# Down projections moved in between the two parts of the input projection, and a last output tile split over two PSUM tiles

## The chip, the cores and the metric

The kernel runs on one NeuronCore of a Trainium2 chip. The metric is the device time of one execution in microseconds (us), the median of several executions on the chip. The profile of one execution gives the start and the length of every instruction on each engine: TensorE (PE, the matmuls; PEld is its weight load), VectorE (DVE), ScalarE (ACT), GpSimd (POOL) and SyncE (SP, which issues most DMAs).

## The reference, cut to what matters

The input x has 2048 tokens of 448 features. It is normalised; one branch is a linear recurrence over the tokens (a diagonal complex state), the other a gated feed-forward layer; the output joins them.

```python
xn = _layernorm(x, axis=-1)
# branch s: Bu = xn @ B_bar (complex); h_t = Lam_bar * h_{t-1} + Bu_t
y = 2.0 * einsum("blp,dp->bld", hseq, Cmat).real + xn * Dskip     # = s
# branch g: w_gate, w_up are 448 x 1792, w_down is 1792 x 448
h = sigmoid(xn @ w_gate) * (xn @ w_up)
g = silu(h @ w_down)
return x + s * g
```

## The kernel before, in words

**Tiling.** The tokens are cut into four chunks c of 512; each chunk has four output tiles j of 128 tokens. Per chunk PE does four kinds of work:

- gate and up (`gu_step`, L688 and L689): 14 steps, one for each of seven 256-wide blocks of w_gate and w_up. The 448 features are contracted as seven slices of 64 rows, and two 64-row matmuls run side by side on the two halves of the array, into the two halves of one `gu` tile. ACT turns a gate tile into `sig` (L702), DVE joins the up tile with it into `hF` (L705).
- the input projection of the recurrence (`b_units`), for four blocks pt of state, taken two at a time. 448 is 3 x 128 + 64, so each block has a 64-row part, the *pairs* (L736 and L737, for pt 3 L739 and L741), and three full-row parts for each of the real and the imaginary half, the *fulls* (L749, L752). All of them add up in one `gu` tile; ACT copies it to `bus` (L760 to L768), and DVE runs the scan on it (`ssm_pair`, L796 to L820; `ssm_stack`, L830 to L850), which gives `hT`.
- the down projection (`down`, L864): 14 full-row matmuls of 448 columns over `hF` of the chunk before, into an `acc` tile; ACT makes `g_t` of it (L870).
- the output of the recurrence (`yout`, L889): seven full-row matmuls over `hT`; then DVE adds the skip term (L895), multiplies with `g_t` (L897), adds x (L899), and SP stores the tile (L901).

Down and output of chunk c - 1 are spread among the gate and up steps of chunk c; those of the last chunk come at the end.

**PSUM.** There are three `gu` tiles of two 2 KB halves each (one for each index of their middle dimension), handed out in turn by `next_gu`, and two `acc` tiles of one half each, handed out in turn by `next_acc`. At the end, when gate and up are through, the six halves of the three `gu` tiles are handed out singly as `free_banks`, the two halves of one tile after each other.

**Order.** Every operation is added to a planner (`Plan`) with an estimated cost and with what it reads and writes. PE's order is that of the program, exactly. For the other engines the planner works out backwards from PE's order when each operation is due, then goes forwards and takes, of what is available, the operation that is due first. So the orders of ACT, DVE, POOL and SP come out of the costs, and they come out anew when PE's order or a cost is changed. Instructions on one engine run in the order in which they were emitted. `SW`, 0.1 us, is the planner's cost of a change between 64-row and full-row matmuls on PE; `first=True` of `down` adds it.

**Names that the change touches.** `b_units(c, pts)` adds one PE operation for the pairs of both blocks, then one for the fulls of each with its ACT copies. `down(c, j, first, bank)` adds one PE operation and the `g_t` operation. `yout(c, j, first, banks, parts)` can cut its 448 columns into parts, each with its own matmuls, DVE operations and store. The calls touched stand in chunk 1 (L974 to L979), chunk 2 (L992 to L998), chunk 3 (L1013 to L1019) and at the very end (L1046). Chunk 0's `b_units` have no `down` to go with.

Of the kernel before, what the change touches and what calls it, by code (L numbers as in the profile page):

```python
# [73 lines left out]
class Plan:  # L74
# [10 lines left out]
    def add(self, eng, cost, fn, r=(), w=(), dma=0, lat=None, chain=False, name="", rate=230e3):  # L85
        o = Op()
        o.idx, o.eng, o.cost, o.fn, o.dma, o.name = len(self.ops), eng, cost, fn, dma, name
        o.lat = LAT.get(eng, 0.0) if lat is None else lat
        o.pre, o.suc, o.rate = {}, [], rate
        o.slot = None  # L90
        if dma and eng != "POOL":
            o.slot, self.n_dma = self.n_dma, self.n_dma + 1
        o.start = o.end = None
        for k in r:
            if k in self.w:
                self._edge(self.w[k], o, True)
        for k in w:
            for q in self.r.get(k, ()):
                self._edge(q, o, False)
            if k in self.w:  # L100
                self._edge(self.w[k], o, True)
        for k in w:
            self.w[k] = o
            self.r[k] = []
        for k in r:
            if k not in w:
                self.r.setdefault(k, []).append(o)
        if chain or eng == "PE" or (eng == "DVE" and self.seq):
            key = ("chain", eng)
            if key in self.last_of:  # L110
                self._edge(self.last_of[key], o, None)
            self.last_of[key] = o
        self.ops.append(o)
        return o
# [131 lines left out]
def kernel(  # L246
# [95 lines left out]
    acc = [pp.tile([P, 512], FP32, name=f"acc{i}") for i in range(2)]  # L342

    pl = Plan(185.0)
    add = pl.add
# [121 lines left out]
    def next_acc():  # L467
        a = acc_n[0] % 2
        acc_n[0] += 1
        return a  # L470
# [29 lines left out]
    def xr(c, lo=0, hi=TPC):  # L500
        return [("xnT", c % 3, j, h) for j in range(lo, hi) for h in "ab"]
# [176 lines left out]
    SW = 0.1  # L678
# [44 lines left out]

    bus_n = [0]

    def b_units(c, pts, last_r=True):
        x = xnT[c % 3]
        slots = [next_gu() for _ in pts]
        bk = [("bT", 0), ("bT", 1), ("bT3", 0), ("bT3", 1), "bT3l"] + (
            [("bT6", 0), ("bT6", 1)] + [("bT6", i, h) for i in range(2) for h in range(2)] if 3 in pts else [])  # L730

        def pairs():
            for pt, a in zip(pts, slots):
                if pt < 3:
                    ps = slice(pt * P, pt * P + P)
                    T.matmul(gu[a][:, 0, :], lhsT=bT[0:H, 3, 0, ps], rhs=x[0:H, 6, :], start=True, stop=False)  # L736
                    T.matmul(gu[a][:, 1, :], lhsT=bT[H:P, 3, 1, ps], rhs=x[H:P, 5, :], start=True, stop=False)  # L737
                else:
                    T.matmul(gu[a][:, 0, 0:256], lhsT=bT6[0:H, 3, :], rhs=x[0:H, 6, 0:256],  # L739
                             start=True, stop=False)  # L740
                    T.matmul(gu[a][:, 1, 0:256], lhsT=bT6[H:P, 3, :], rhs=x[H:P, 5, 256:512],  # L741
                             start=True, stop=False)
        add("PE", 0.216 * len(pts), pairs, r=xr(c) + bk, w=[("gu", a) for a in slots], name=f"bp{c}.{pts[0]}")
        for n, (pt, a) in enumerate(zip(pts, slots)):
            def fulls(pt=pt, a=a):
                for i in range(2):
                    for kt in range(3):
                        if pt < 3:
                            T.matmul(gu[a][:, i, :], lhsT=bT[:, kt, i, pt * P:pt * P + P], rhs=x[:, 2 * kt, :],  # L749
                                     start=False, stop=(kt == 2))  # L750
                        else:
                            T.matmul(gu[a][:, i, 0:256], lhsT=bT6[:, kt, :],  # L752
                                     rhs=x[:, 2 * kt, i * 256:i * 256 + 256], start=False, stop=(kt == 2))
            add("PE", (6 * 0.215 if pt < 3 else 6 * 0.11) + (0 if n else SW), fulls,
                r=xr(c) + bk + [("gu", a)], w=[("gu", a)], name=f"b{c}.{pt}")
            u = bus_n[0] % NBUS
            bus_n[0] += 1
            bus_of[c, pt] = u
            if pt < 3:
                add("ACT", act(1024), lambda u=u, a=a: A.copy(out=bus[u][:], in_=gu[a][:]),  # L760
                    r=[("gu", a)], w=[("bus", u)])
            else:
                h2 = lambda t: t.rearrange("p (i n) -> p i n", i=2)
                add("ACT", act(512), lambda u=u, a=a: A.copy(out=h2(bus[u][:, 0, :]), in_=gu[a][:, :, 0:256]),
                    r=[("gu", a)], w=[("bus", u)])
                add("ACT", 0.6, lambda u=u, a=a: A.copy(out=h2(bus[u][0:H, 1, :]), in_=gu[a][H:P, :, 0:256]),
                    r=[("gu", a)], w=[("bus", u, 1)])
                add("ACT", 0.6, lambda u=u, a=a: A.copy(out=h2(bus[u][H:P, 1, :]), in_=gu[a][0:H, :, 0:256]),  # L768
                    r=[("gu", a)], w=[("bus", u, 2)])
# [87 lines left out]
    def down(c, j, first=False, bank=None):  # L857
        key, d = bank if bank else (lambda a: (("acc", a), acc[a][:, 0:D]))(next_acc())
        js = slice(j * P, j * P + P)

        def f():
            for ft in range(FT):
                m, h = ft % 7, ft // 7
                T.matmul(d, lhsT=hF[c % 2][:, m, h, js], rhs=wd[:, ft, :], start=(ft == 0), stop=(ft == FT - 1))  # L864
        add("PE", 14 * 0.189 + (SW if first else 0), f, r=[("wd", 0), ("wd", 1)] + [("hF", c % 2, m) for m in range(7)], w=[key],
            name=f"d{c}.{j}")
        g = gt_n[0] % NGT
        gt_n[0] += 1
        gt_of[c, j] = g
        add("ACT", act(448), lambda: A.activation(g_t[g][:], d, ACT.Silu, scale=0.5), r=[key, "silutab"], w=[("gt", g)])  # L870
# [4 lines left out]
    def yout(c, j, first=False, banks=None, parts=((0, D),)):  # L875
        js = slice(j * P, j * P + P)
        t = c * TPC + j
        g = gt_of[c, j]
        o = o_n[0] % NO
        o_n[0] += 1  # L880
        q = t % NXD
        xq = xd[q][:]
        for pi, (c0, c1) in enumerate(parts):
            key, y = banks[pi] if banks else (lambda a: (("acc", a), acc[a][:, 0:D]))(next_acc())
            y = y[:, 0:c1 - c0]

            def f(y=y, c0=c0, c1=c1):
                for i, (hm, cm) in enumerate(K_ORDER):
                    T.matmul(y, lhsT=hT[c % 2][:, hm, js], rhs=cT[:, cm, c0:c1], start=(i == 0), stop=(i == 6))  # L889
            n = c1 - c0  # L890
            add("PE", 7 * (0.004 + n / 2400.0) + (SW if first else 0), f,
                r=cTk + [("hT", c % 2, p) for p in range(4)], w=[key], name=f"y{c}.{j}")
            ok = ("o", o, pi)
            od = o_t[o][:, c0:c1]
            add("DVE", dve1(n), lambda od=od, y=y, c0=c0, c1=c1: V.tensor_tensor(out=od, in0=y, in1=xq[:, c0:c1], op=ALU.add),  # L895
                r=[key, ("xd", q)], w=[ok])
            add("DVE", dve2(n), lambda od=od, c0=c0, c1=c1: V.tensor_tensor(out=od, in0=od, in1=g_t[g][:, c0:c1], op=ALU.mult),  # L897
                r=[ok, ("gt", g)], w=[ok])
            add("DVE", dve2(n), lambda od=od, c0=c0, c1=c1: V.tensor_tensor(out=od, in0=od, in1=x_all[:, t, c0:c1], op=ALU.add),  # L899
                r=[ok, ("x", t)], w=[ok])  # L900
            add("SP", 0.45, lambda od=od, c0=c0, c1=c1: Q.dma_start(out=out_flat[t * P:(t + 1) * P, c0:c1], in_=od),  # L901
                r=[ok], w=[("store", t, pi)], dma=n * 256)
# [68 lines left out]
    halves(1, 2)  # L971
    gu_step(1, 2)
    prepare(2)
    b_units(1, (0, 1))  # L974
    down(0, 0)
    for i in range(3, 6):
        gu_step(1, i, i == 3)
    b_units(1, (2, 3))
    down(0, 1)  # L979
    for i in range(6, 12):  # L980
        gu_step(1, i, i == 6)
    down(0, 2, True)
# [6 lines left out]

    for i in range(0, 4):  # L990
        gu_step(2, i)
    b_units(2, (0, 1))  # L992
    down(1, 0)
    yout(0, 2)
    for i in range(4, 7):
        gu_step(2, i, i == 4)
    b_units(2, (2, 3))
    down(1, 1)  # L998
    yout(0, 3)
    prepare(3)  # L1000
    for i in range(7, 12):
# [8 lines left out]

    for i in range(0, 4):
        gu_step(3, i)
    b_units(3, (0, 1))  # L1013
    down(2, 0)
    yout(1, 2)
    for i in range(4, 7):
        gu_step(3, i, i == 4)
    b_units(3, (2, 3))
    down(2, 1)  # L1019
    yout(1, 3)  # L1020
    for i in range(7, 12):
        gu_step(3, i, i == 7)
# [20 lines left out]
    down(3, 2, bank=free_banks[2])  # L1043
    yout(3, 2)
    down(3, 3, bank=free_banks[3])
    yout(3, 3, banks=[free_banks[4], free_banks[5]], parts=((0, 256), (256, 448)))  # L1046

    pl.solve({"g0.0": 5.9})
    with tc.manual_schedule():
# [33 lines left out]
```

## Time and profile before

| | |
|---|---|
| median of 4 runs | 190.05 us (189.2 to 190.36) |
| the profiled execution | 189.6 us, its span (first to last instruction) 187.8 us |
| granted TensorE clock, mean | 0.998 |
| PE busy | 181.1 us, 96% of the span |
| DVE busy | 168.4 us, 90% |
| ACT busy | 87.6 us, 47% |
| POOL busy | 32.7 us, 17% |

How to read it: PE's matmuls overlap, so that the length printed for one (0.38 us for 512 columns) is longer than the distance to the next (0.22 us); sums are made with the distances. "x14" in a row is a merged run of 14 instructions. The share of busy time is a mean over the span; which engine sets the end has to be read from the chain of waits and from the idle time in front of the instructions. In a row, "[0.20 <-DVE hF L705]" means that the engine stood idle for 0.20 us before it and that this ended with an operation of DVE's line 705.

### The profile page before, as it was taken

To read this page: it belongs to the slowest core of one execution; us is meant where nothing else is said; L and a number is where in the kernel's file an instruction comes from. 1 tells how busy PE (TensorE), PEld (TensorE's weight loads), DVE (VectorE), ACT (ScalarE), POOL (GpSimd) and SP (SyncE) were. 2 spreads that over 40 slices of the span, in tenths; PEclk is the share of its full clock that TensorE was granted. 3 is DMA by queue.
4 is the path that set the end of the run, shared out by engine and by line. 5 is a ranking of instruction groups with operands and counts; after the bars stand their busy time and mean duration, and the time that the engine had idled before them with its cause. 6 is when DMAs were issued, how large, how long until landed. Compare 5 with 4: busy or idle time off the path is not lost.

```text
span 187.8 us, 3507 instructions
## 1 busy us (share of the span) xinstructions
PE 181.1 (96%) x1375; PEld 89.8 (48%) x1375; DVE 168.4 (90%) x303; ACT 87.6 (47%) x124; POOL 32.7 (17%) x84
## 2 busy tenths in 40 slices
PE   7999999999999999999999999999999999999990
PEld 2585554474454444444454445444445445455560
DVE  3765799997999999999999998999999999899943
ACT  3469997734988751244547331237146221502110
POOL 3163466000005560000027800000000000000000
PEclk9999999999999999999999999999999999999999
DMA  5999999599500033200000343000000100000220
GB/s 126 266 217 239 167 140 210 112 249 130 187 3 0 0 72 78 49 0 3 0 2 0 77 101 70 0 28 0 24 3 0 49 0 28 0 24 28 73 77 24
DMA packets 29239, 13.43 MB, mean 71 GB/s; under 512 B 19619, under 2 KB 29222, under 8 KB 29222
## 3 DMA queue, kind: packets, MB, share of 16 engines
q1 hardware_dynamic: 27878, 12.05, 31.6%
q10 hardware_dynamic: 1344, 1.15, 2.3%
q8 instruction: 11, 0.18, 0.4%
q14 instruction: 6, 0.05, 0.1%
HBM read 6.77 MB, written 1.84 MB: 46 GB/s over the span
## 4 chain that ended last, share of the span: by engine, by line
PE 80%; DMA 8%; DVE 7%; issue 1%; POOL 1%; SPq 1%; ACT 1%; DVEq 0%
PE gu L688 33%; PE acc L864 17%; PE acc L889 11%; PE gu L749 9%; PE gu L864 6%; DMA x_all<-in_A_x_dram 5%; DVE hF L705 3%; DMA wG<-in_B_w_gate_dram 3%; PE gu L752 1%; PE gu L736 1%; DVE bst L421 1%; SPq L351 1%; POOL sdb L436 1%; PE gu L889 1%; PE gu L689 1%
## 5 line engine op out<-in xcount | busy, mean ns | idle before, releaser
L688 PE MATMUL gu<-xnT,wG 64*128 64x512 bf16 (+1 forms) x224 | 46.4, 349 | 0.3 <-DVE xnT L489 0.3
L689 PE MATMUL gu<-xnT,wG 64*128 64x512 bf16 (+1 forms) x224 | 46.4, 350 | 0.0
L688 PE MATMUL gu<-xnT,wU 64*128 64x512 bf16 (+1 forms) x203 | 46.2, 369 | 0.2 <-ACT sig L702 0.2
L689 PE MATMUL gu<-xnT,wU 64*128 64x512 bf16 (+1 forms) x203 | 46.2, 369 | 0.0
L702 ACT ACTIVATE sig<-gu 128x1024 f32<-128x1024 f32 x21 | 21.3, 1021 | 32.0 <-PE gu L689 29.7
L864 PE MATMUL acc<-wd,hF 128*128 128x448 bf16 x168 | 33.8, 353 | 0.0
L864 PEld LDWEIGHTS <-hF 128*128 128x128 bf16 x224 | 21.7, 98 | 20.9 <-issue 1.3
L688 PEld LDWEIGHTS <-wG 64*128 64x128 bf16 x224 | 20.4, 94 | 21.1 <-issue 3.0
L688 PEld LDWEIGHTS <-wU 64*128 64x128 bf16 x203 | 18.8, 94 | 22.1 <-issue 1.3
L705 DVE SCALAR_TENSOR_TENSOR hF<-sig,gu 128x1024 bf16<-128x1024 f32 x21 | 25.5, 1214 | 1.5 <-PE gu L689 1.1
L803 DVE TENSOR_TENSOR_SCAN wv<-c_r,st,z 128x512 bf16<-128x512 f32 x18 | 23.0, 1275 | 0.0
L889 PE MATMUL acc<-cT,hT 128*128 128x448 bf16 x105 | 22.0, 353 | 0.0
L689 PEld LDWEIGHTS <-wG 64*128 64x128 bf16 x224 | 20.3, 94 | 0.2
L689 PEld LDWEIGHTS <-wU 64*128 64x128 bf16 x203 | 18.7, 94 | 0.5 <-issue 0.5
L749 PE MATMUL gu<-xnT,bT 128*128 128x512 bf16 x72 | 16.9, 380 | 0.0
L760 ACT CAST bus<-gu 128x1024 bf16<-128x1024 f32 x12 | 12.1, 1010 | 9.3 <-PE gu L749 9.0
L889 PEld LDWEIGHTS <-hT 128*128 128x128 bf16 x119 | 11.5, 98 | 10.1 <-issue 0.4
L870 ACT ACTIVATE g_t<-acc 128x448 bf16<-128x448 f32 x12 | 6.5, 538 | 17.6 <-PE acc L864 17.6
L435 POOL TENSOR_SCALAR veb<-mv 128x2 bf16<-128x2 bf16 (+1 forms) x5 | 3.8, 754 | 55.3 <-DVE mv L422 55.2
L421 DVE BATCH_NORM_STATS2 bst<-x_all 128x6 f32<-128x448 bf16 x16 | 9.4, 613 | 3.6 <-DMA x_all<-in_A_x_dram 3.6
L454 ACT ACTIVATE xn<-x_all,nmr,rsd 128x448 bf16<-128x448 bf16 x12 | 8.4, 764 | 6.0 <-POOL nmr L444 5.9
L864 PE MATMUL gu<-wd,hF 128*128 128x448 bf16 x56 | 11.1, 352 | 0.0
(132 smaller groups left out, 245.4 us busy)
## 6 DMA issues: line engine op xcount, KB each, us to landing
out_dram<-o_t SPq DMA_DIRECT2D x15, 112.0 KB, 1.7
wd<-in_B_w_down_dram SPq DMA_DIRECT2D x2, 784.0 KB, 5.5
x_all<-in_A_x_dram SPq DMA_DIRECT2D x3, 448.0 KB, 4.5
wU<-in_B_w_up_dram SPq DMA_DIRECT2D x2, 448.0 KB, 11.4
wU<-in_B_w_up_dram SPq DMA_DIRECT2D x2, 336.0 KB, 7.1
wG<-in_B_w_gate_dram SPq DMA_DIRECT2D x1, 448.0 KB, 8.3
wG<-in_B_w_gate_dram ACTq DMA_DIRECT2D x1, 448.0 KB
xnT<-xn SPq DMA_TRANSPOSE x24, 2.4
```

The source lines that it names most:

```text
L421: add("DVE", 0.6, lambda: V.bn_stats(out=bst[b][:], in_=x_all[:, t, :]), r=[("x", t)], w=[("bst", b)])
L454: add("ACT", 0.65, lambda: A.activation(xn[b][:, 0:448], x_all[:, t, :], ACT.Identity, bias=nmr[:, t, :], scale=rsd[:, t, :]), r=[("x", t) ...
L688: T.matmul(gu[a][:, 0, ts], lhsT=w_[0:H, s, ms], rhs=x[0:H, s, ts], start=(s == 0), stop=(s == 6))
L689: T.matmul(gu[a][:, 1, ts], lhsT=w_[H:P, (s + 1) % 7, ms], rhs=x[H:P, s, ts], start=(s == 0), stop=(s == 6))
L702: add("ACT", act(1024), lambda: A.activation(th, gu[a][:], ACT.Tanh, scale=0.5), r=[("gu", a)], w=[tk])
L705: add("DVE", dve1(1024), lambda: V.scalar_tensor_tensor(out=ho, in0=th, scalar=1.0, in1=gu[a][:], op0=ALU.add, op1=ALU.mult), r=[("gu", a) ...
L749: T.matmul(gu[a][:, i, :], lhsT=bT[:, kt, i, pt * P:pt * P + P], rhs=x[:, 2 * kt, :], start=False, stop=(kt == 2))
L760: add("ACT", act(1024), lambda u=u, a=a: A.copy(out=bus[u][:], in_=gu[a][:]), r=[("gu", a)], w=[("bus", u)])
L803: dve(1.194, lambda k=k: V.tensor_tensor_scan(out=wv[:, k, :], data0=rb, data1=z[:, k, :], initial=(st[pt][:, k, :] if c else 0.0), op0=AL ...
L864: T.matmul(d, lhsT=hF[c % 2][:, m, h, js], rhs=wd[:, ft, :], start=(ft == 0), stop=(ft == FT - 1))
L870: add("ACT", act(448), lambda: A.activation(g_t[g][:], d, ACT.Silu, scale=0.5), r=[key, "silutab"], w=[("gt", g)])
L889: T.matmul(y, lhsT=hT[c % 2][:, hm, js], rhs=cT[:, cm, c0:c1], start=(i == 0), stop=(i == 6))
```

## The change

`b_units` takes a function `mid` and calls it between the pairs and the fulls. In chunks 1, 2 and 3 the two `down` calls that stood behind `b_units` become this `mid`. Between the pairs and the fulls of the same blocks there are then 14 full-row matmuls into an `acc` tile; the planner's cost of the mode change goes from the first fulls to this `down`. An argument that nothing used goes away. The outputs `yout` that stand behind a `down` in chunks 2 and 3 stay where they are, behind the fulls.

Apart from that, the very last output tile: its two parts were columns 0 to 255 and 256 to 447 in the two halves of one `gu` tile; they become columns 0 to 127 in the next `acc` tile and columns 128 to 447 in the first half of that `gu` tile.

```diff
-    def b_units(c, pts, last_r=True):
+    def b_units(c, pts, mid=None):
...
         add("PE", 0.216 * len(pts), pairs, r=xr(c) + bk, w=[("gu", a) for a in slots], name=f"bp{c}.{pts[0]}")
+        if mid:
+            mid()
         for n, (pt, a) in enumerate(zip(pts, slots)):
...
-            add("PE", (6 * 0.215 if pt < 3 else 6 * 0.11) + (0 if n else SW), fulls,
+            add("PE", (6 * 0.215 if pt < 3 else 6 * 0.11) + (0 if n or mid else SW), fulls,
...
-    b_units(1, (0, 1))
-    down(0, 0)
+    b_units(1, (0, 1), lambda: down(0, 0, True))
     for i in range(3, 6):
         gu_step(1, i, i == 3)
-    b_units(1, (2, 3))
-    down(0, 1)
+    b_units(1, (2, 3), lambda: down(0, 1, True))
...
-    b_units(2, (0, 1))
-    down(1, 0)
+    b_units(2, (0, 1), lambda: down(1, 0, True))
     yout(0, 2)
...
-    b_units(2, (2, 3))
-    down(1, 1)
+    b_units(2, (2, 3), lambda: down(1, 1, True))
     yout(0, 3)
...
-    b_units(3, (0, 1))
-    down(2, 0)
+    b_units(3, (0, 1), lambda: down(2, 0, True))
     yout(1, 2)
...
-    b_units(3, (2, 3))
-    down(2, 1)
+    b_units(3, (2, 3), lambda: down(2, 1, True))
     yout(1, 3)
...
-    yout(3, 3, banks=[free_banks[4], free_banks[5]], parts=((0, 256), (256, 448)))
+    a = next_acc()
+    yout(3, 3, banks=[(("acc", a), acc[a]), free_banks[4]], parts=((0, 128), (128, 448)))
```

## The prediction

> **What bounds the kernel now.** First the page's busy line, then the sum of PE's waits.
>
> ```profile
> PE 181.1 (96%) x1375; PEld 89.8 (48%) x1375; DVE 168.4 (90%) x303; ACT 87.6 (47%) x124; POOL 32.7 (17%) x84
> ```
> ```profile
> PE gu L736 <- DVE hF L705: 0.5, 2, 0.3
> PE gu L688 <- ACT sig L702: 0.2, 1, 0.2
> ```
>
> Past the first 10 us PE has 0.7 us of waits in all: it sets the pace, and only something that shortens PE's own stream, or what comes behind its last matmul, can shorten the kernel. So the third view is the end of the chain of waits, and the timeline beside it.
>
> ```profile
> 179.23 2.65 PE gu L864 x14
> 181.88 1.36 PE gu L889 x14
> 183.26 0.44 DVE o_t L895
> 183.79 0.30 DVE o_t L897
> 184.11 0.29 DVE o_t L899
> 184.41 0.28 DVE o_t L895
> 184.71 0.27 DVE o_t L897
> 185.00 0.26 DVE o_t L899
> ```
> ```profile
> 172.65 0.98 ACT L870 ACTIVATE g_t<-gu 128x448 bf16<-128x448 f32 x2 [8.47 <-PE gu L864]
> ...
> 179.36 0.62 DVE L895 TENSOR_TENSOR o_t<-acc,xd 128x448 bf16<-128x448 f32 x1
> ...
> 181.72 1.51 PE L889 MATMUL gu<-cT,hT 128*128 128x256 bf16 x14
> ...
> 183.26 0.42 DVE L895 TENSOR_TENSOR o_t<-gu,xd 128x256 bf16<-128x256 f32 x1 [2.36 <-PE gu L889]
> ```
>
> The reader is to see that DVE, idle for 2.36 us, takes up part one of the last tile only when *both* parts' 14 matmuls are through, and then does six operations in a row (183.26 to 185.26) with nothing beside them.
>
> **Part two of the change, the last tile.** Is that wait due to the shared tile? Two other rows say so: the two `g_t` of downs (3,0) and (3,1), also in two halves of one `gu` tile, both start at 172.65, when the second down is through; and L895 of tile (3,2), in a tile of its own, starts at 179.36 while PE is already 0.3 us into the next down. Here a rule speaks against the change: the Trainium skill ("PSUM — Partial Sum Buffer", Summary: rules for kernel authors) asks of a read during matmuls only that it be in a different bank. The halves already are two banks, so by the rule DVE could start early now and the new tile brings 0. The rows show the wait at tile grain; I follow them.
>
> The sum needs three durations at new widths. Matmul distance: 448 columns 2.65 / 14 = 0.189 us; 256 columns 0.109 (the starts 8.20, 8.31, 8.41 of the first gate step); a line through both gives 0.136 at 320 and 0.056 at 128 (six 128-column transposes in 0.51 us, the last one 0.24 of it: 0.054). L895: 0.62 at 448, 0.42 at 256, 0.35 at 192, so 0.28 at 128 and 0.49 at 320. L897 and L899: 0.38, 0.29, 0.26, so 0.23 and 0.32. Between dependent DVE operations lie 0.03 to 0.04, and 0.11 after part one's L895.
>
> - PE: part one 181.72 + 7 x 0.056 = 182.11; part two + 7 x 0.136 = 183.06. Now it is 181.72 + 7 x 0.109 + 7 x 0.083, 183.06 too, as the columns are as many. DVE starts 0.20 later (183.26).
> - DVE, part one: 182.31, + 0.28 + 0.11 + 0.23 + 0.03 + 0.23 = 183.19, all beside part two's matmuls. `g_t`, needed at 182.70, is there at 181.91 + 0.54 = 182.45.
> - DVE, part two: 183.26, when PE releases it; + 0.49 + 0.04 + 0.32 + 0.03 + 0.32 = 184.46. Now 185.26: **0.80 earlier**.
> - The last store is 80 KB instead of 48 KB. The DMA rows give 1.5 us from issue to landing for 48 KB, 1.6 for 64, 1.7 for 112: **0.1 later**. A second rule: "DMA: Bandwidth & Descriptors" (Specifications) wants 512 B per descriptor at least; rows of the last store go from 384 B to 640 B, so the rule would make it cheaper, while the rows show a longer landing with more bytes across that line. I take the rows. Part one's store (32 KB) is issued at about 183.2 and SP is free of it 0.33 us later, before 184.46.
>
> Sum: -0.70 us, with -0.55 if L895's release takes longer, -0.8 if the landing doesn't grow.
>
> **Part one of the change, the moved downs.** From the timeline of chunk 2:
>
> ```profile
> 84.11 0.38 PE L736 MATMUL gu<-xnT,bT 64*128 64x512 bf16 x1
> ...
> 84.33 0.38 PE L736 MATMUL gu<-xnT,bT 64*128 64x512 bf16 x1
> ...
> 84.64 2.76 PE L749 MATMUL gu<-xnT,bT 128*128 128x512 bf16 x12
> ...
> 87.24 2.81 PE L864 MATMUL acc<-wd,hF 128*128 128x448 bf16 x14
> ...
> 89.89 1.49 PE L889 MATMUL acc<-cT,hT 128*128 128x448 bf16 x7
> ```
>
> Pair to pair is 0.22, pair to full 0.31: the change of mode costs 0.09, once. A down behind 64-row matmuls pays the same elsewhere: the chain has 2.75 for those and 2.65 for a down behind full rows. So the 0.09 moves from the fulls to the down; after it all stay full-row, and the way back into 64 rows is paid once, as now. Six places times 0. The 12 fulls take 2.60 = 12 x 0.217, with no hole between a pair and the full that adds to the same half: no stall that the down could fill. PE's stream gets no shorter.
>
> Waits that the new places could add:
> - *The down, 2.6 us earlier* (2.0 in the second groups). It needs all seven `hF`: the last L705 of each chunk before ends at 38.99, 80.03 and 122.9, the new downs start at 42.8, 84.6 and 128.0. Covered by 3.8 us or more. Their `g_t` on ACT come earlier; ACT is busy 47%.
> - *The fulls, 2.65 us later*, and so their ACT copies. They free the `gu` tiles. Tightest is chunk 1's second group, with no output tile behind: fulls of 1.30 and 0.65, then gate and up steps of 1.51. The second step reuses pt 2's tile 2.25 us after its fulls (mode change included), and the copy takes 0.2 + 1.0; the third reuses pt 3's 3.1 us after its own, and its three copies (0.59, 0.58, 0.58) are done some 2.4 after. Cover 0.7 to 1.0 us. ACT has other work there (two 0.6 us `wv` copies, a 0.67 us `ctmp`); if the planner puts one of these first, PE waits 0 to 0.5 us, once.
> - *The scan on DVE reads `bus`.* In chunks 1 and 2 the first new `bus` (ready at 45.3 and 87.2) waits 25 and 14 us for its L796 (70.9 and 101.8), whatever the delay. In chunk 3 it is close: the first copy ends at 130.51 and is read at 133.75. 2.65 later it ends at 133.16: cover 0.6 us.
>
> ```profile
> 129.50 1.01 ACT L760 CAST bus<-gu 128x1024 bf16<-128x1024 f32 x1 [1.04 <-PE gu L749]
> ...
> 133.75 0.69 DVE L796 TENSOR_TENSOR ta<-bus,cosT 128x1024 bf16<-128x1024 bf16 x1
> ```
>
> What if it is not covered? DVE's backlog ends at L895 of tile (2,2), 171.51 to 172.13, whose `acc` tile PE needs at 172.45: about 0.25 us, plus 0.54 that DVE stood idle before L705 at 164.67. DVE can lose 0.8 us before PE waits.
>
> Both ends for the moved downs: +0.5 (a chunk-1 wait) and -0.4 (the stalls at 42.47 and 108.72, 0.2 each, gone by a new order; the one at 30.3 lies before the first moved step). I take 0, the row being a stream without holes.
>
> **Sum:** 189.6 - 0.7 = 188.9 for an execution like the profiled one. That one lies 0.45 below the median of the runs, so on their median **189.35**, say 189.3.
>
> **Rivals.**
> 1. *The order drawn anew also loses the two 0.2 us stalls:* -1.1, 188.95. For it: those are orders of ACT and DVE that came out badly and are worked out again. Against: as many can come in.
> 2. *Slower: DVE starves in chunk 3.* All `bus` tiles of that chunk come 2.65 us later and DVE's order is fixed; if it stands idle that long in front of L796, 2.65 - 0.8 = 1.85 reaches PE at tile (3,0), less 0.7 from the tail: +1.15, 191.2. It decides once DVE loses more than 1.5 us. For it: DVE is busy 90% and has holes of only some 1.1 us between 130 and 170. Against: the cover of 0.6, and work of chunk 2 that can go first.
> 3. *Part two's DVE work waits for part one's store,* as both lie in one `o_t` tile: the store lands at about 184.75, then 1.20 on DVE, so 185.95 instead of 185.26, +0.1 for the bytes: +0.8, 190.85. Against: the statistics of the first x tile start at 3.14 while another transfer into the same x_all, issued at 1.2 and 2.7 under way, is in flight; but that is a read behind a write, not a write behind a read.
> 4. *The tile isn't what part one waits for:* the six operations stay in a row, 190.05.
>
> **How the numbers follow.** Forecast (tail alone) 0.49; rival 1 0.25; rival 2 0.13; rival 3 0.08; rival 4 0.05. The median of four runs spans 0.6%, so 0.5%, 0.95 us, is about what can be told from no change. The forecast's -0.7 lies within it; with 0.4 us either way from the new order, more than a third of its chance lies beyond. Faster: 0.19 + 0.21 = 0.40. Slower: rival 2 and half of rival 3 and a little, 0.18. The same: 0.42. The range goes from 188.4 (rival 1 with 0.5 more) to 190.9 (rival 3), which leaves out rival 2.
>
> **What would show it.** Right: L895 of the last tile starts near 182.3 on the old time axis for part one and right behind PE's last matmul for part two, L901's last issue is 0.8 us earlier measured from PE's last matmul; 0.31 from pair to down, 0.19 from down to full. Wrong: idle DVE before L796 of chunk 3, PE waits on ACT's L760 to L768 in chunk 1, part two's L895 starting with a landing of L901, or PE's last matmul at another time than 183 by more than 0.5 us.

## The result, and the profile after

The changed kernel takes 189.14 us (median of 37 executions), the kernel before 189.81 us (median of 56; the 190.05 shown ahead was that of the first four). The ratio is 0.9971, with a 95% interval from 0.9957 to 0.9984: 0.3% faster, between 0.3 and 0.8 us. The profiled execution took 189.17 us, its span is 187.4 us.

In the changed source the lines behind `b_units` have moved down by two: L749 is L751, L864 is L866, L889 is L891, L895 to L901 are L897 to L903. First PE's waits in the changed kernel, without the 1.2 us in front of its first matmul, then the end of its chain of waits.

```profile
PE gu L688 <- DMA wG<-in_B_w_gate_dram: 0.5, 1, 0.5
PE gu L688 <- ACT sig L702: 0.2, 1, 0.2
PE gu L736 <- DVE hF L705: 0.2, 1, 0.2
```
```profile
179.51 2.65 PE gu L866 x14
182.16 0.39 PE acc L891 x7
182.55 0.96 PE gu L891 x7
183.54 0.50 DVE o_t L897
184.07 0.34 DVE o_t L899
184.43 0.32 DVE o_t L901
```

Three DVE operations instead of six lie behind the last matmul. The timeline shows where the other three went (start, length, operation, and in brackets the idle time before):

```profile
182.00 0.55 PE L891 MATMUL acc<-cT,hT 128*128 128x128 bf16 x7
...
182.39 1.11 PE L891 MATMUL gu<-cT,hT 128*128 128x320 bf16 x7
182.59 0.29 DVE L897 TENSOR_TENSOR o_t<-acc,xd 128x128 bf16<-128x128 f32 x1 [1.05 <-PE acc L891]
182.99 0.23 DVE L899 TENSOR_TENSOR o_t<-o_t,g_t 128x128 bf16<-128x128 bf16 x1
183.25 0.22 DVE L901 TENSOR_TENSOR o_t<-o_t,x_all 128x128 bf16<-128x128 bf16 x1
183.54 0.49 DVE L897 TENSOR_TENSOR o_t<-gu,xd 128x320 bf16<-128x320 f32 x1
```

Part one's L897 starts 0.59 us after the tile's first matmul (before: 1.54) and runs beside part two's matmuls; DVE is through 2.75 us after that first matmul (184.75 less 182.00), before 3.54 (185.26 less 181.72). That is 0.79 us. The last store takes 1.6 us to land instead of 1.5.

The middle is as long as it was: from the second pair of chunk 1 to the last tile's first matmul 139.26 us (42.74 to 182.00), before 139.25 (42.47 to 181.72). The span shrank by 0.44 us only, because the head of this execution was 0.27 us longer: chunk 0's second pairs start at 33.59 us, before at 33.32. The head differs from execution to execution of one kernel, so the experiments below are also read without it: from chunk 0's second pairs (about 33 us) to the start of the last matmul, and from there to the end of DVE.

### The profile page after: what moved, and what is told of

Same layout as the page of the kernel before. It is cut to its first block, busy times and chain, and to the rows that moved or that the text cites. A ratio compares the mean times of both kernels' runs of the same rounds, so it can differ in the third digit from the quotient of the medians.

```text
span 187.4 us, 3508 instructions
## 1 busy us (share of the span) xinstructions
PE 181.5 (97%) x1375; PEld 89.7 (48%) x1375; DVE 168.6 (90%) x303; ACT 87.6 (47%) x124; POOL 32.8 (17%) x84
## 4 chain that ended last, share of the span: by engine, by line
PE 91%; DMA 4%; DVE 2%; ACT 1%; SPq 0%; issue 0%; DVEq 0%
PE gu L688 42%; PE acc L866 17%; PE acc L891 11%; PE gu L751 8%; PE gu L866 6%; DMA wG<-in_B_w_gate_dram 4%; PE gu L689 3%; PE gu L736 1%; PE gu L754 1%; DVE hF L705 1%; PE gu L891 1%; ACT sig L702 0%; PE acc L481 0%; ACT xn L454 0%; SPq L351 0%; DVE ta L832 0%
## 5 line engine op out<-in xcount | busy, mean ns | idle before, releaser
L866 PE MATMUL acc<-wd,hF 128*128 128x448 bf16 x168 | 33.8, 353 | 0.0
L866 PEld LDWEIGHTS <-hF 128*128 128x128 bf16 x224 | 21.2, 98 | 22.0 <-issue 3.2
L891 PE MATMUL acc<-cT,hT 128*128 128x448 bf16 (+1 forms) x112 | 22.6, 344 | 0.0
L751 PE MATMUL gu<-xnT,bT 128*128 128x512 bf16 x72 | 16.9, 379 | 0.0
L891 PEld LDWEIGHTS <-hT 128*128 128x128 bf16 x119 | 11.3, 98 | 10.0 <-issue 0.4
L762 ACT CAST bus<-gu 128x1024 bf16<-128x1024 f32 x12 | 12.1, 1007 | 5.6 <-PE gu L751 5.3
L435 POOL TENSOR_SCALAR veb<-mv 128x2 bf16<-128x2 bf16 (+1 forms) x5 | 3.3, 666 | 59.0 <-DVE mv L422 59.0
L897 DVE TENSOR_TENSOR o_t<-acc,xd 128x448 bf16<-128x448 f32 (+1 forms) x16 | 9.6, 598 | 2.8 <-PE acc L891 2.3
L866 PE MATMUL gu<-wd,hF 128*128 128x448 bf16 x56 | 11.1, 352 | 0.0
```

## The experiments

Ratios are to the kernel before, timed on the same chip beside it. "Stretch" is the time from the first of chunk 0's second pairs to the start of the last matmul, "tail" that from there to the end of DVE's last operation, both from differences of starts in the trace.

| kernel | median, us | ratio (95% interval) | stretch | tail |
|---|---|---|---|---|
| before | 189.81 | 1 | 149.66 | 2.29 |
| changed | 189.14 | 0.9971 (0.9957 to 0.9984) | 149.62 | 1.54 |
| e10, changed once more | 189.15 | 0.9966 (0.9949 to 0.9983) | 149.49 | 1.55 |
| e1, last tile only | 189.05 | 0.9953 (0.9925 to 0.9981) | 149.60 | 1.54 |
| e2, downs only | 189.86 | 0.9992 (0.9976 to 1.0008) | 149.68 | 2.28 |
| e3, tiles only | 189.21 | 0.9960 (0.9934 to 0.9986) | 149.65 | 1.70 |
| e4, widths only | 189.77 | 0.9995 (0.9976 to 1.0013) | 149.60 | 2.33 |
| e5, downs ahead of pairs | 189.80 | 0.9999 (0.9971 to 1.0027) | 150.37 | 1.55 |
| e6, later bus | 188.99 | 0.9942 (0.9923 to 0.9960) | 149.62 | 1.55 |
| e7, sum formed early | 189.38 | 0.9966 (0.9948 to 0.9984) | 149.66 | 1.67 |
| e8, for two tiles | 188.76 | 0.9936 (0.9911 to 0.9961) | 149.70 | 1.24 |
| e11, e8 once more | 188.79 | 0.9963 (0.9940 to 0.9985) | 149.71 | 1.24 |
| e9, e8 with one down ahead | 189.54 | 0.9975 (0.9955 to 0.9995) | 149.49 | 1.24 |
| e12, e9 once more | 189.16 | 0.9974 (0.9948 to 1.0000) | 149.57 | 1.24 |

### The two halves of the change, apart

e1 is the kernel before with the last tile's edit alone:

```diff
-    yout(3, 3, banks=[free_banks[4], free_banks[5]], parts=((0, 256), (256, 448)))
+    a = next_acc()
+    yout(3, 3, banks=[(("acc", a), acc[a]), free_banks[4]], parts=((0, 128), (128, 448)))
```

> The kernel before with the last tile's new parts and tiles only (128 columns in an acc tile, 320 in a gu half); no down is moved. Theory (all of the change's gain is in the last tile): 0.7 us less than before, ratio 0.9963; DVE's first L895 of the last tile 0.20 us behind part one's last matmul, end of DVE's last operation 1.40 us behind the start of the last matmul slot's end, instead of 2.20. Rival (the moved downs bring the gain): ratio 1.000.

e2 is the changed kernel with this edit taken back; the six downs stay moved.

> The changed kernel with the old last tile (256 and 192 columns in the two halves of one gu tile): only the six downs are moved. Theory (PE's stream has the same mode changes and no holes to fill): ratio 1.000, within 0.002; the two stalls of PE before L736 in chunk 1 and before L688 at 108.7 stay. Rival (the downs bring 0.3%): 0.997. Rival (late bus copies starve DVE): 1.002 or more.

e1 has the changed kernel's tail and its gain; e2 has the tail of before, a ratio whose interval holds 1, and PE's two later waits where they were. The whole gain is in the last tile; the moved downs bring nothing that can be seen, in the time or in the stretch. From the end of the last matmul's slot (0.14 us after its start in e1, 0.08 before) the tails are 1.41 and 2.20 us, as expected.

### The tile or the widths?

e3 keeps 256 and 192 columns, in separate tiles; e4 takes 128 and 320, in the two halves of one tile (both against the kernel before):

```diff
-    yout(3, 3, banks=[free_banks[4], free_banks[5]], parts=((0, 256), (256, 448)))
+    a = next_acc()
+    yout(3, 3, banks=[(("acc", a), acc[a]), free_banks[4]], parts=((0, 256), (256, 448)))
```
```diff
-    yout(3, 3, banks=[free_banks[4], free_banks[5]], parts=((0, 256), (256, 448)))
+    yout(3, 3, banks=[free_banks[4], free_banks[5]], parts=((0, 128), (128, 448)))
```

> The kernel before with the last tile's parts still 256 and 192 columns wide, but in an acc tile and a gu half. Theory (the wait for the shared tile is what costs): part one's L895 starts near 0.76 + 0.20 us after the first matmul of the tile, DVE ends about 0.58 us earlier than before, ratio 0.997. Rival (the narrower first part is what helps): 1.000.

> The kernel before with parts of 128 and 320 columns, still in the two halves of one gu tile. Theory: part one's L895 waits for part two's last matmul as before, DVE's six operations stay in a row with nearly the same sum, the last store is 80 KB instead of 48 KB: 0 to 0.15 us slower, ratio 1.000 to 1.001. Rival (the split helps by itself): 0.997.

The last tile's matmuls and the first DVE operation in e3, then in e4:

```profile
181.57 0.93 PE L889 MATMUL acc<-cT,hT 128*128 128x256 bf16 x7
...
182.53 0.42 DVE L895 TENSOR_TENSOR o_t<-acc,xd 128x256 bf16<-128x256 f32 x1 [1.79 <-PE acc L889]
```
```profile
182.34 1.50 PE L889 MATMUL gu<-cT,hT 128*128 128x128 bf16 x14
...
183.89 0.29 DVE L895 TENSOR_TENSOR o_t<-gu,xd 128x128 bf16<-128x128 f32 x1 [2.37 <-PE gu L889]
```

In e3, whose DVE ends 0.58 us earlier than before as worked out, DVE starts 0.96 us after the first matmul, with part one; in e4 1.55 us after it, with part two, although part one ends 0.4 us after the start. So it is the shared tile that makes DVE wait, and the narrow first part is worth nothing without the second tile. Sharing alone is not enough, though. Downs (3,2) and (3,3) of the kernel before also lie in the two halves of one `gu` tile, and the `g_t` of (3,2) does not wait for the second:

```profile
177.94 0.54 ACT L870 ACTIVATE g_t<-gu 128x448 bf16<-128x448 f32 x1 [4.32 <-PE gu L864]
...
179.07 2.81 PE L864 MATMUL gu<-wd,hF 128*128 128x448 bf16 x14
```

There an output tile stands between the two downs; where DVE waited, PE's matmuls for both halves follow each other directly.

With the second tile, the narrow first part is worth 0.16 us of DVE time (tails 1.70 and 1.54), of which the longer landing of 80 KB takes back 0.08 (from issue to the wait's end 1.52 us in e3, 1.60 in the changed kernel).

### The place of the down

e5 puts each of the six downs ahead of the pairs:

```diff
+        if mid:
+            mid()
-        add("PE", 0.216 * len(pts), pairs, r=xr(c) + bk, w=[("gu", a) for a in slots], name=f"bp{c}.{pts[0]}")
-        if mid:
-            mid()
+        add("PE", 0.216 * len(pts) + (SW if mid else 0), pairs, r=xr(c) + bk, w=[("gu", a) for a in slots], name=f"bp{c}.{pts[0]}")
...
-            add("PE", (6 * 0.215 if pt < 3 else 6 * 0.11) + (0 if n or mid else SW), fulls,
+            add("PE", (6 * 0.215 if pt < 3 else 6 * 0.11) + (0 if n else SW), fulls,
```

> The changed kernel with each of the six moved downs ahead of the pairs instead of behind them, so that PE goes 64-row, down, pairs, fulls. Theory (a change between 64-row and full-row matmuls costs 0.09 each way, and the place between pairs and fulls is free only because it adds none): two changes more at six places, +1.12 us, less the stall of about 0.3 before chunk 1's second pair, which the down now covers: +0.8 us against the changed kernel, so about 0.1 slower than before, ratio 1.0005. Rival (place doesn't matter): as the changed kernel, 0.9965.

```profile
86.43 2.82 PE L866 MATMUL acc<-wd,hF 128*128 128x448 bf16 x14
89.19 0.39 PE L736 MATMUL gu<-xnT,bT 64*128 64x512 bf16 x1
...
89.41 0.38 PE L736 MATMUL gu<-xnT,bT 64*128 64x512 bf16 x1
...
89.73 2.76 PE L751 MATMUL gu<-xnT,bT 128*128 128x512 bf16 x12
```

This is the timeline of e5 in chunk 2. Down to pair is 2.76 us instead of 14 x 0.189 = 2.65; pair to full is 0.32 instead of 0.22. Each crossing costs 0.1 us, and in e5 there are twelve more of them. Its stretch is 0.75 us longer than the changed kernel's: 12 x 0.095 = 1.14, less a hole of 0.36 between the pairs of chunk 1 that the down covered, less another of 0.36 (at 109.0 us in the changed kernel) that is not there in e5, plus a new one of 0.19 at 80.5 us. In both kernels the distance right after each crossing is 0.011 us longer than the later ones (all 21 crossings of the changed kernel's stretch, all 33 of e5's), which adds 12 x 0.011 = 0.13. That makes 0.74. The place between pairs and fulls is free because PE crosses there anyway.

### How much delay the bus copies bear

e6 puts, in chunk 3, the output tiles (1,2) and (1,3) between pairs and fulls as well:

```diff
-    b_units(3, (0, 1), lambda: down(2, 0, True))
-    yout(1, 2)
+    b_units(3, (0, 1), lambda: (down(2, 0, True), yout(1, 2)))
...
-    b_units(3, (2, 3), lambda: down(2, 1, True))
-    yout(1, 3)
+    b_units(3, (2, 3), lambda: (down(2, 1, True), yout(1, 3)))
```

> The changed kernel with, in chunk 3, the output tiles (1,2) and (1,3) also put between pairs and fulls, so that chunk 3's bus copies come another 1.3 us later than in the changed kernel, past the 0.6 us of cover before L798. Theory: DVE idles up to 0.7 us in chunk 3 unless other work goes first, and its cushion of 0.8 us before PE waits at tile (3,0) takes that: as the changed kernel, ratio 0.9965 within 0.001. Rival (DVE has no cushion): 0.7 us longer than the changed kernel, ratio 1.000.

```profile
133.48 1.01 ACT L762 CAST bus<-gu 128x1024 bf16<-128x1024 f32 x1 [2.08 <-PE gu L751]
...
135.08 0.67 DVE L798 TENSOR_TENSOR ta<-bus,cosT 128x1024 bf16<-128x1024 bf16 x1
```

The copy ends at 134.49, L798 starts 0.6 us later, and DVE has no hole there: the planner's new order let other DVE work go first. So the cushion was not put to the test; what the run shows is that a further delay of 1.3 us costs nothing, stretch and tail being those of the changed kernel. The ratio, 0.9942, is below the 0.9965 within 0.001 that was expected, but not for a reason in these two; in the profiled executions e6's stretch begins 0.28 us earlier, and the interval (0.9923 to 0.9960) still touches the changed kernel's.

### A shorter end

e7 moves down (3,3) ahead of tile (3,2), so that `g_t` is there early, and lets DVE form skip x `g_t` + x for the last tile beforehand. Behind the matmuls two operations are left per part:

```diff
+        if pre:
+            add("DVE", dve2(D), lambda: V.tensor_tensor(out=xq, in0=xq, in1=g_t[g][:], op=ALU.mult),
+                r=[("xd", q), ("gt", g)], w=[("xd", q)])
+            add("DVE", dve2(D), lambda: V.tensor_tensor(out=xq, in0=xq, in1=x_all[:, t, :], op=ALU.add),
+                r=[("xd", q), ("x", t)], w=[("xd", q)])
...
+            if pre:
+                add("DVE", dve1(n), lambda od=od, y=y, c0=c0, c1=c1: V.tensor_tensor(out=od, in0=y, in1=g_t[g][:, c0:c1], op=ALU.mult),
+                    r=[key, ("gt", g)], w=[ok])
+                add("DVE", dve2(n), lambda od=od, c0=c0, c1=c1: V.tensor_tensor(out=od, in0=od, in1=xq[:, c0:c1], op=ALU.add),
+                    r=[ok, ("xd", q)], w=[ok])
...
-    yout(3, 2)
-    down(3, 3, bank=free_banks[3])
+    down(3, 3, bank=free_banks[4])
+    yout(3, 2)
     a = next_acc()
-    yout(3, 3, banks=[(("acc", a), acc[a]), free_banks[4]], parts=((0, 128), (128, 448)))
+    yout(3, 3, banks=[(("acc", a), acc[a]), free_banks[3]], parts=((0, 192), (192, 448)), pre=True)
```

> The changed kernel with another end: down (3,3) ahead of output tile (3,2), so that its g_t is there early; DVE forms skip times g_t plus x for the last tile while it would idle; behind the last matmuls only two DVE operations are left for each part (times g_t, plus the sum), parts of 192 and 256 columns. Theory (the end is what lies behind the last matmul): part two 0.42 + 0.04 + 0.29 instead of 0.49 + 0.04 + 0.32 + 0.03 + 0.32, so 0.45 us less than the changed kernel, 1.1 less than before, ratio 0.994. Rival (the end is set by the stores, not by DVE): as the changed kernel.

It missed: the tail is 1.67 us, not the 1.1 expected. The timeline of e7 shows why.

```profile
182.22 0.62 DVE L910 TENSOR_TENSOR o_t<-acc,xd 128x448 bf16<-128x448 f32 x1
...
182.88 0.39 DVE L912 TENSOR_TENSOR o_t<-o_t,g_t 128x448 bf16<-128x448 bf16 x1
183.30 0.39 DVE L914 TENSOR_TENSOR o_t<-o_t,x_all 128x448 bf16<-128x448 bf16 x1
183.61 0.35 DVE L903 TENSOR_TENSOR o_t<-acc,g_t 128x192 bf16<-128x192 f32 x1
```

The three operations of tile (3,2), 1.4 us, used to run beside the down that came after it. That down had been moved away, so they now stood in front of the last tile. e8 gives tile (3,2) the early sum too (`yout(3, 2, pre=True)`); e11 is e8 once more, e10 the changed kernel.

> As e7_pre_sum, and output tile (3,2) gets the same treatment (skip times g_t plus x formed early, two DVE operations behind its matmuls). Theory (in e7 the four DVE operations still owed to tile (3,2), which a down had hidden before, stood in front of the last tile): (3,2) needs 0.62 + 0.04 + 0.39 on DVE instead of 1.40, so the last DVE operation ends 0.3 us earlier than in the changed kernel, 1.2 to 1.25 us behind the start of the last matmul instead of 1.54; ratio to before 0.9945 to 0.996. Rival (the end is set by something other than DVE): 1.5 us behind the last matmul as in the changed kernel, ratio 0.997.

> The kernel of e8_pre_sum_both once more. Theory (its gain is behind the last matmul and is there in every execution): last DVE operation 1.24 us behind the start of the last matmul, ratio to before 0.994 to 0.9955. Rival (the low median of e8's six runs was luck of the first weight loads): 0.9965 as the changed kernel.

> The changed kernel once more, on the chip of these runs: ratio 0.9965, last DVE operation 1.54 us behind the start of the last matmul.

Both times the tail is 1.24 us, 0.31 less than the changed kernel's 1.54 and 1.55, as worked out; e8's ratio 0.9936 (of six executions) and e11's 0.9963 are both below 1 with their intervals. Against the changed kernel's 0.9971 and 0.9966 the gain of 0.16% is not resolved by the times: the intervals overlap, and e11's median ratio lies where its rival had it. That this version beats the kernel before is shown, that it beats the changed one only by its tail in the trace.

e9 is e8 with down (0,0) ahead of its pairs, e12 is e9 once more:

```diff
-    b_units(1, (0, 1), lambda: down(0, 0, True))
+    down(0, 0, True)
+    b_units(1, (0, 1))
```

> As e8_pre_sum_both, and down (0,0) alone stands ahead of its pairs (as all six did in e5_down_first). Theory: the hole of 0.36 us between the first and the second pair of chunk 1 goes, two mode changes of 0.095 come: 0.17 us less than e8_pre_sum_both between chunk 0's second pairs and the last matmul. Rival (the hole moves to another place): no less.

> The kernel of e9_first_down_ahead once more. Theory (its slow median came from the first 34 us, in which weights land at different times, not from the moved down): 149.5 us again from chunk 0's second pairs to the last matmul, ratio 0.993 to 0.995 like e11. Rival (the new order that the planner makes of chunk 0 costs about 1 us there in most executions): ratio 0.997 again, second pairs of chunk 0 later than 34 us on the trace.

PE's waits in e9, then in e12, the same kernel:

```profile
PE gu L688 <- DMA wG<-in_B_w_gate_dram: 1.3, 1, 1.3
...
PE gu L736 <- DVE hF L705: 1.0, 1, 1.0
```
```profile
PE gu L688 <- DMA wG<-in_B_w_gate_dram: 0.6, 1, 0.6
PE gu L688 <- ACT sig L702: 0.2, 1, 0.2
```

The 1.0 us in front of L736 in e9 lies in chunk 0, at 31.7 us, ahead of the stretch. The stretch is 0.21 us shorter in e9 than in e8 and 0.14 shorter in e12 than in e11 (worked out: 0.17), and the hole between chunk 1's pairs is gone. That is little more than the 0.13 by which the two executions of the changed kernel differ. The medians don't follow: 0.9975 and 0.9974, no better than the changed kernel, where 0.993 to 0.995 had been expected of e12. e9's profiled execution is at chunk 0's second pairs 1.5 us later than e12's (34.7 and 33.2 us), so of the rival's two signs for e12 the ratio of 0.997 came, and the late head did not. The planner draws chunk 0's orders on ACT and DVE anew as well, and whether that makes late heads more frequent stays open.

## Why the prediction was right, step by step

- **The tail, -0.70 us.** Each term of the sum came out: part one's first DVE operation 0.59 us after the tile's first matmul (worked out 0.59), the end of DVE 2.75 us after it (2.74), the landing 0.08 longer (0.1). From the tile's first matmul to the end of the span it is 5.39 us instead of 6.12, 0.73 less (0.70). Durations at new widths, taken from a line through the old ones, were within 0.01 us: 0.29, 0.23, 0.22 at 128 columns, 0.49, 0.32, 0.32 at 320. The medians differ by 0.67 us; that they come so close is in part luck, as the interval reaches from 0.3 to 0.8.
- **The wait is at tile grain, not at bank grain.** e4 (two banks, one tile, DVE waits) and e3 (two tiles, it doesn't) show it directly. The bank rule of the Trainium skill ("PSUM — Partial Sum Buffer", Summary: rules for kernel authors) says what the memory allows; the semaphores of this program asked for more.
- **The larger rows of the last store make it no cheaper.** 48 KB in 384 B rows landed in 1.52 us, 64 KB in 512 B rows (e8) in 1.56, 80 KB in 640 B rows in 1.60: even steps with the bytes and none at 512 B, though bytes and rows grew together and were not tested apart. The rule of 512 B (the Trainium skill, "DMA: Bandwidth & Descriptors", Specifications) is stated there for line rate, and 80 KB in 1.60 us is 51 GB/s, where the loads in the head of this kernel ran at over 200 GB/s for a while. So a rule for line rate need not hold for such a store, and the prediction did well to take the rows.
- **The moved downs, 0.** e2 (0.9992, 0.9976 to 1.0008) and the unchanged stretch show it, and e5 the reason, the number of mode changes: 21 in the stretch before and after, 33 in e5. The possible wait of up to 0.5 us in chunk 1 did not come: no wait on the copies (now L762 to L770) is in PE's list.
- **The cover of 0.6 us in chunk 3** was exact: in the changed kernel the first copy ends at 133.44 and is read at 134.04.
- **The rivals.** The two waits stayed (rival 1). Their size was misread: the list counts idle time behind the printed lengths, 0.2 us each, but from start to start they took 0.57 and 0.58 us instead of 0.22 (42.47 and 108.72 in the kernel before), so each costs 0.36 and rival 1 would have brought 0.7 instead of 0.4. DVE did not starve (rival 2), but the 0.8 us that it was said to be able to lose were never tested. Part two's L897 starts at 183.54, 0.07 us after part one's last operation ends, when part one's store can't have landed yet (rival 3). The tile was what part one waited for (rival 4).
- **Too wide** was the room given to the planner's new orders, 0.4 us either way: in the stretch, all kernels with six free or unmoved downs lie within 0.22 us. And the base of 190.05 was 0.24 above what 56 executions gave: 189.81 less 0.70 is 189.11, against 189.14 measured.

## What to carry to other kernels

Look behind the last matmul: an engine that stands idle there and then works alone is time on the path, also in a kernel whose TensorE is busy 96% of the span. Where a reader waits for a writer's later, unrelated work, ask whether both lie in one tile, before changing widths; two banks alone did not part them here. Before moving work, count what it crosses (mode changes) and what ran under its cover: e7 took away a down that had hidden 1.4 us of DVE work, and lost with it what it had won.

## What the runs showed of the hardware that was not expected

The head scatters more than anything that was changed here. The same kernel reached chunk 0's second pairs at 34.7 us in one profiled execution and at 33.2 us in another (e9 and e12); PE's wait for the first gate weights went from nothing (before) to 1.3 us (e9), with the same transfers issued in the same order in both. That wait alone does not tell how late the head is: the changed kernel waited 0.5 us in one execution and 1.0 in the other (e10), and the second was at chunk 0's second pairs earlier, at 33.24 us instead of 33.59. From there to the last matmul two executions of one kernel differ by 0.01 to 0.13 us (e8 and e11, the changed kernel and e10), and their tails by 0.01 at most. So e8's 0.31 us is seen at once in its tail, and not in the whole times of 6 and 12 executions.
